# Parity attention: a power moved behind the first copies, z weight loads in step 0, output products from step 8

## The chip, the cores and the metric

The kernel runs on one core of a Trainium2 chip. The metric is device time in microseconds, the median of the runs shown. Engines: TensorE (PE), VectorE (DVE), ScalarE (ACT), GpSimd (POOL) and SyncE (SP). SP and POOL here also issue most of the DMAs, each in the order of its own instructions; ACT issues a few.

## The reference, cut to what matters

x has 2048 rows of 576 numbers (bf16). Four layers, A B A B, each adds its result to x:

```python
# A: 32 heads of 18; position p sees p, p-2, ..., p-14
qkv = layernorm(x) @ wqkv
attn = softmax(mask(q . k[p - 2w], w = 0..7) * 18**-0.5)
x = x + (attn @ v) @ wo
# B: gMLP
z = gelu(layernorm(x) @ w_in)                 # 576 -> 4608, halves z1, z2
g = w_sp @ layernorm(z2) + b_sp               # mixes the 2048 rows
x = x + (z1 * g) @ w_out
```

## The kernel before

The rows of x are handled by parity: even rows first, then odd rows, so that attention at distance 2 is attention at distance 1. Row block i has 128 rows; there are NS = 16.

**Layer A** (`layer_A`, L332) has a preparation and a loop of NST = 34 steps. Everything in it is written in order by hand (`manual_schedule`, L363): each engine, and SP and POOL as DMA queues, carries out its instructions in the order in which the code names them.

- Preparation, first layer (li = 0, L554 to L670): per row block S_ takes mean and variance on DVE, R_ (L594) adds epsilon on DVE and takes the power -1/2 on POOL (L597), A_ (L600) normalises on DVE, T_ (L615) transposes into xnT by a DMA on SP (T_pe: on PE for the first four). VW (L391) makes a piece of V. PG (L402) makes one projection of q or k for 128 columns d and 512 rows cc; it goes to a staging buffer, and when a buffer (d, 1024 rows) is complete, 8 copies by DMA (L439) put its heads into QK. `queues` tells which of SP and POOL issues a copy: they take turns for d = 0 and 4, and POOL has two of three for the others (q2, L551). In the first layer the staging of d = 3 and 4 for the first 1024 rows is borrowed from `win2a` (lent, L362), into which the z weights are loaded later. `fill_window_rows` (L194) writes the window pattern into QK on DVE.
- Before the loop come six more PG (`pre`), L_mm(0), EXP(0) and, in the first layer, two VW (L750 to L759).
- Step s of the loop (L760) does L_mm(s+1) (logits of half of a tile's heads, PE), EXP(s+1) (ACT, L462), PV(s) (PE, L476; then DVE L482, L483), and then what a table holds for step s. Tile t has two steps, 2t and 2t+1. There are 17 tiles: 128 rows, then 120 each. After the second step the tile's output o_t is transposed by a DMA on SP: odd tiles and tile 0 straight into the ring oT (L489), the other even tiles into a slot (L493), from which O_CP (L502, DVE) copies into the ring.
- The table is filled by `at(step, function)`, and within a step the order is that of the calls. PG and VW that are left; O_CP; XO (loads the residual rows, SP); WO(i, half) (output product, PE L530; addition, DVE L533); LN_STATS and LN_XN (statistics on DVE, then POOL: L231, L232, L252, L255); XST and XN_ST (stores of x and of the normalised rows, SP); LN_T (loads rows transposed into xnT, SP, L549; two for each block i from 8 on).
- `lag`, `twice` and `units` (L717 to L720) say in which steps the WO halves stand: one in each step from `lag` on, two in the steps of `twice`. `wo_steps[i]` are the two steps of block i; O_CP, XO, LN_STATS and so on get their steps from it (L722 to L740). `vsteps` (L712) are the steps of the VW that are left.
- In the first layer the output weights wo (`load_wo`, SP) are loaded in step 2 and the first three quarters of the z weights (`load_win2a`, six pieces, POOL) in steps 3, 5, ..., 13 (L741 to L744). The rest, win2b, goes in steps 16 to 26 (POOL).

In the third layer (li = 2) wqk, wv, wo and win2a are already loaded during the layer before.

**Layer B** (`layer_B`, L778) makes z2 by row blocks from xnT (z_mm, L836), then the gate products (L984) and the output products (L1033). Its first z products stand on PE among the last WO of layer A.

Of the kernel before, what the change touches and what calls it, by code (L numbers as in the profile page):

```python
# [63 lines left out]
class K:  # L64
# [267 lines left out]
    def layer_A(self, li):  # L332
        nc, tc, cfg = self.nc, self.tc, self.cfg
# [57 lines left out]
        def VW(t, hh, dve):  # L391
            nk = tdim(t)[0]
            pv = self.PT_tile([P, 512], f32, "pv")
            for c in range(5):
                nc.tensor.matmul(pv[:nk, 0:288], lhsT=self.xnT[:, c, k0_(t):k0_(t) + nk],  # L395
                                 rhs=wv_sb[:, c, hh * 288:(hh + 1) * 288], start=(c == 0), stop=(c == 4))
            evac(v_ext[:nk, t, 16 * hh:16 * hh + 16, 0:DH], pv[:nk, 0:288].rearrange("p (b d) -> p b d", d=DH), dve)
# [43 lines left out]
        NST = 2 * NT  # L441
# [112 lines left out]
        if li == 0:  # L554
# [39 lines left out]
            def R_(i0, n):  # L594
                rs = rstds[:, i0:i0 + n]
                nc.vector.tensor_scalar_add(out=rs, in0=mvs[:, i0:i0 + n, 1], scalar1=EPS)
                nc.gpsimd.tensor_tensor(out=rs, in0=rs, in1=self.neg_half[:, 0:1].to_broadcast([P, n]), op=ALU.pow)  # L597
            xns = {}

            def A_(*tiles):  # L600
                for i in tiles:
                    xns[i] = xn = self.xn_bufs[self.xn_rr % len(self.xn_bufs)]
                    self.xn_rr += 1
                    nc.vector.tensor_scalar(out=xn[:, 0:D], in0=xts[i], scalar1=mvs[:, i, 0:1],
                                            scalar2=rstds[:, i:i + 1], op0=ALU.subtract, op1=ALU.mult)
# [54 lines left out]
            for k_, (d, cc) in enumerate(order):  # L660
                for qk in ((1, 0) if d < 4 else (0,)):
                    PG(d, qk, cc, False, (nc.gpsimd, nc.sync) if d in (0, 4) else q2)
                if k_ == 3:
                    R_(12, 4)
                    VW(3, 0, False)
                    VW(3, 1, False)
                if k_ == 4:
                    A_(12, 13, 14, 15)
            T_(12, 13, 14, 15)
            nvw0, nvw = 4, 9  # L670
# [28 lines left out]
        def at(s, f, *a):  # L699
            table.setdefault(s, []).append((f, a))  # L700
        pgs = [(d, qk, cc) for d, cc in ((0, 2), (1, 2), (2, 2), (0, 3), (1, 3), (2, 3), (3, 2), (3, 3), (4, 2), (4, 3))
               for qk in ((1, 0) if d < 4 else (0,))]
        PG_END = 14
# [4 lines left out]
        if li == 0:  # L708
            at(0, VW, *vws[0], True)
            at(13, VW, *vws[1], True)  # L710
            vws = vws[2:]
        vsteps = ([x for x in range(PG_END, NST) if x not in (18, 23, 28)] if li == 0 else  # L712
                  [x for x in range(3, NST) if x not in (18, 23, 28)])
        for k_, (t, hh) in enumerate(vws):
            assert vsteps[k_] <= 2 * t - 2 + hh
            at(vsteps[k_], VW, t, hh, vsteps[k_] >= PG_END and k_ % 2 == 0)
        lag = 10 if li == 0 else 9  # L717
        twice = (18, 23, 28, 31) if li == 0 else (18, 23, 28)
        units = [x for x in range(lag, NST) for _ in range(2 if x in twice else 1)]
        wo_steps = list(zip(units[0::2], units[1::2])) + [(NST, NST), (NST + 1, NST + 2)]  # L720
        assert len(wo_steps) == NS
# [17 lines left out]
                    at(s1 + 5, LN_T, 2 * i - NS + k_)  # L739
        at(2 * (NT - 3) + 3, O_CP, NT - 3)  # L740
        if li == 0:  # L741
            at(2, self.load_wo, nc.sync)
            for k_, f in enumerate(reversed(self.load_win2a(nc.gpsimd))):
                at(3 + 2 * k_, f)  # L744
        at(PG_END + 2, alloc_win2b)
        for k_ in range(6):
            at(PG_END + 2 + 2 * k_, win2b_piece, k_)
# [397 lines left out]
```

## Time and profile before

| | us |
|---|---|
| median of 3 runs | 1187.06 |
| lowest and highest | 1185.82, 1187.1 |
| the profiled execution, its own time | 1185.85 |
| its span | 1184.1 |

The span runs from the first to the last instruction of the profiled execution. Its PE is busy for 1166.3 us of it, DVE for 552.9, ACT for 339.6 and POOL for 281.1. The mean granted clock of PE is 0.994 of full speed. A row of a timeline names start, duration, engine, line, operation, what is written and read, how many instructions are merged, and in brackets the idle time before the first and what ended it. "SPq" and "POOL ... DMA_DIRECT2D" are instructions that issue DMAs.

### The profile page before, as it was taken

To read this page: it belongs to the slowest core of one execution; us is meant where nothing else is said; L and a number is where in the kernel's file an instruction comes from. 1 tells how busy PE (TensorE), PEld (TensorE's weight loads), DVE (VectorE), ACT (ScalarE), POOL (GpSimd) and SP (SyncE) were. 2 spreads that over 40 slices of the span, in tenths; PEclk is the share of its full clock that TensorE was granted. 3 is DMA by queue.
4 is the path that set the end of the run, shared out by engine and by line. 5 is a ranking of instruction groups with operands and counts; after the bars stand their busy time and mean duration, and the time that the engine had idled before them with its cause. 6 is when DMAs were issued, how large, how long until landed. Compare 5 with 4: busy or idle time off the path is not lost.

```text
span 1184.1 us, 20070 instructions
## 1 busy us (share of the span) xinstructions
PE 1166.3 (99%) x8258; PEld 620.1 (52%) x8258; DVE 552.9 (47%) x1137; ACT 339.6 (29%) x491; POOL 281.1 (24%) x411
## 2 busy tenths in 40 slices
PE   8899999999999999999999999999999999999998
PEld 5457544444444444447755674444444444444677
DVE  9568788432332232334554787873332233232322
ACT  5478554211101111101247884550111110111000
POOL 3559955100000000001135598550000000000000
PEclk9999899999999999999999999999999999999999
DMA  8699997000000000049636797940000000001332
GB/s 196 108 191 251 211 203 162 23 12 12 1 12 12 12 12 1 1 138 281 178 88 120 180 251 192 244 91 13 12 12 12 12 1 12 12 1 40 114 106 73
DMA packets 182800, 106.44 MB, mean 90 GB/s; under 512 B 134938, under 2 KB 164042, under 8 KB 182709
## 3 DMA queue, kind: packets, MB, share of 16 engines
q1 hardware_dynamic: 170117, 84.54, 30.6%
q0 software_dynamic: 6240, 14.88, 4.9%
q10 hardware_dynamic: 6352, 5.75, 1.6%
q8 instruction: 64, 1.05, 0.4%
q14 instruction: 27, 0.22, 0.1%
HBM read 42.40 MB, written 21.77 MB: 54 GB/s over the span
## 4 chain that ended last, share of the span: by engine, by line
PE 89%; DMA 3%; POOL 3%; DVE 3%; issue 1%; ACT 0%; DVEq 0%; POOLq 0%; SPq 0%
PE pg L984 42%; PE po L1033 12%; PE pz L836 6%; PE pz L960 6%; PE pz1s L960 6%; PE pzs L836 6%; PE pp L418 4%; PE pw L530 2%; PE pv L395 2%; PE L_ps L453 2%; POOL ln_xn L252 2%; PE O_ps L476 2%; DMA o_slot<-o_t 1%; DVE ln_st L591 1%; POOL QK L78 1%
## 5 line engine op out<-in xcount | busy, mean ns | idle before, releaser
L984 PE MATMUL pg<-Wq,Z 128*128 128x512 bf16 x2304 | 500.2, 379 | 0.0
L984 PEld LDWEIGHTS <-Z 128*128 128x128 bf16 x2304 | 225.4, 98 | 271.9
L988 DVE TENSOR_TENSOR g_tmp<-pg,ln_xn 128x512 f32<-128x512 f32 x144 | 99.6, 692 | 421.6 <-PE pg L984 421.6
L979 ACT ACTIVATE z1T<-pz 128x1024 bf16<-128x1024 f32 x36 | 34.9, 1021 | 500.2 <-PE pz L960 500.2
L78 POOL DMA_DIRECT2D wout<-in_B_w_out_dram x4 | 4.3, 1067 | 598.8 <-PE pg L984 598.8
L1033 PE MATMUL po<-wout,Z 128*128 128x288 bf16 x1152 | 141.4, 286 | 0.0
L462 ACT ACTIVATE P_sb<-L_ps 128x960 bf16<-128x960 f32 (+1 forms) x136 | 125.2, 971 | 39.4 <-PE L_ps L453 38.8
L1033 PEld LDWEIGHTS <-Z 128*128 128x128 bf16 x1152 | 112.7, 98 | 28.8
L836 PEld LDWEIGHTS <-xnT 128*128 128x128 bf16 (+1 forms) x800 | 68.2, 97 | 77.4 <-issue 9.7
L989 DVE TENSOR_TENSOR Z<-g_tmp,z1T 128x512 bf16<-128x512 f32 x144 | 99.7, 692 | 12.2
L885 DVE BATCH_NORM_STATS2 z_st<-zp 128x6 f32<-128x512 bf16 (+1 forms) x160 | 91.7, 619 | 20.8 <-ACT zp L883 20.6
L960 PEld LDWEIGHTS <-w 128*128 128x128 bf16 (+1 forms) x640 | 53.7, 97 | 74.0 <-issue 13.6
L418 PE MATMUL pp<-xnT,wqk_sb 128*128 128x512 bf16 x360 | 83.7, 383 | 2.0 <-DVE o_t L483 2.0
L252 POOL TENSOR_SCALAR ln_xn<-x_new,ln_mv,ln_rstd 128x576 bf16<-128x576 f32 x32 | 73.6, 2299 | 3.0
L1043 DVE TENSOR_TENSOR x_new<-po,xo 128x288 f32<-128x288 f32 (+1 forms) x64 | 28.8, 456 | 87.7 <-PE po L1033 83.9
L960 PE MATMUL pz<-xnT,w 128*128 128x512 bf16 (+1 forms) x320 | 66.5, 380 | 0.0
L960 PE MATMUL pz1s<-xnT,w 128*128 128x512 bf16 (+1 forms) x320 | 66.5, 379 | 0.0
L836 PE MATMUL pz<-win2a,xnT 128*128 128x512 bf16 (+1 forms) x240 | 60.4, 359 | 3.0 <-DMA xnT<-xn_rows 2.7
L78 POOL DMA_DIRECT2D QK<-stg x80 | 48.1, 604 | 52.6 <-DVE stg L387 23.6
L836 PE MATMUL pzs<-win2a,xnT 128*128 128x512 bf16 (+1 forms) x240 | 59.5, 358 | 0.0
L909 POOL TENSOR_SCALAR Z<-zp,z_mv,z_rstd 128x256 bf16<-128x256 bf16 x32 | 54.5, 1704 | 3.4
L883 ACT ACTIVATE zp<-pz 128x1024 bf16<-128x1024 f32 (+2 forms) x56 | 36.6, 720 | 62.9 <-PE pz L836 62.9
(107 smaller groups left out, 957.9 us busy)
## 6 DMA issues: line engine op xcount, KB each, us to landing
xres<-x_new SPq DMA_DIRECT2D x48, 288.0 KB
xo<-xres SPq DMA_DIRECT2D x32, 288.0 KB
wout<-in_B_w_out_dram POOLq DMA_DIRECT2D x4, 1296.0 KB, 8.1
xn_rows<-ln_xn SPq DMA_DIRECT2D x32, 160.0 KB
xo<-xres SPq DMA_DIRECT2D x8, 576.0 KB
w<-in_B_w_in_dram SPq DMA_DIRECT2D x16, 256.0 KB
QK<-stg POOLq DMA_DIRECT2D x52, 72.0 KB, 4.6
QK<-stg SPq DMA_DIRECT2D x42, 72.0 KB
```

The costliest lines, as they stand in the source:

```text
L78: return eng.dma_start(out=out, in_=in_)
L252: e.tensor_scalar(out=xn[:nrows, 0:D], in0=x_t[:nrows, :], scalar1=mv[:nrows, 0:1], scalar2=rstd[:nrows, 0:1], op0=ALU.subtract, op1=ALU.mult)
L418: nc.tensor.matmul(pp[:, :], lhsT=w, rhs=self.xnT[:, c, cc * 512:(cc + 1) * 512], start=(c == 0), stop=(c == 4))
L462: nc.scalar.activation(out=P_bufs[(2 * s + jp) % 4][:nk, :, :, 0:nq], in_=Lv[:nk, :, :, 0:nq], func=ACT.Exp, scale=scale)
L836: nc.tensor.matmul(out[:, o0:o0 + n], lhsT=self.xnT[r0:r1, c, r * P:(r + 1) * P], rhs=win2(c)[r0:r1, w0:w0 + n], start=start, stop=stop, t ...
L885: nc.vector.bn_stats(out=st[:, x // 512, :], in_=zp[:, x:x + min(512, w0 + n - x)])
L909: eng.tensor_scalar(out=Z[:, b0:b1, i, :], in0=zv[:, b0:b1, :], scalar1=mv[:, 0:1], scalar2=rstd[:, 0:1], op0=ALU.subtract, op1=ALU.mult)
L960: nc.tensor.matmul(outs[a_], lhsT=w1[r0:r1, c, sub * P:(sub + 1) * P], rhs=self.xnT[r0:r1, c, q * 512:(q + 1) * 512], start=start, stop=st ...
L984: nc.tensor.matmul(pg[:, :], lhsT=Z[:, jj, i, sub * P:(sub + 1) * P], rhs=Wq[q][:, i, :], start=(i == 0), stop=(i == NS - 1))
L988: nc.vector.tensor_tensor(out=tmp[:], in0=pg[:, :], in1=bsp[:, qs], op=ALU.add)
L989: nc.vector.tensor_tensor(out=uT(jj)[:, sub, qs], in0=tmp[:], in1=z1Ts[jj, sub][:, qs], op=ALU.mult)
L1033: nc.tensor.matmul(acc[hh], lhsT=u_rows(j, i), rhs=wouts[j // NJH][:, j % NJH, hh * 288:(hh + 1) * 288], start=(j == 0), stop=(j == NJ - 1))
```

## The change

Three edits in `layer_A`:

1. First layer: the power of row blocks 12 to 15 (R_) moves from behind the PGs of order 3 to behind those of order 5, that is behind the copies of d = 0 and d = 1, and their normalisation A_ from order 4 to order 5.
2. First layer: wo and all six pieces of win2a are loaded in step 0 and no longer in steps 2 to 13.
3. Both layers: `lag` is 8 (was 10 in the first layer, 9 in the third), and `twice` is steps 18 and 23 (was 18, 23, 28 and 31; 18, 23, 28). So the output products of block i stand in other steps, and with them O_CP, XO, the normalisation, the stores and LN_T. Step 28 takes a VW again.

The steps of the output products that come out of `wo_steps`:

| block | 0 | 1 | 2 | 3 | 4 | 5 | 6 | 7 | 8 | 9 | 10 | 11 | 12 | 13 |
|---|---|---|---|---|---|---|---|---|---|---|---|---|---|---|
| before, first layer | 10, 11 | 12, 13 | 14, 15 | 16, 17 | 18, 18 | 19, 20 | 21, 22 | 23, 23 | 24, 25 | 26, 27 | 28, 28 | 29, 30 | 31, 31 | 32, 33 |
| before, third layer | 9, 10 | 11, 12 | 13, 14 | 15, 16 | 17, 18 | 18, 19 | 20, 21 | 22, 23 | 23, 24 | 25, 26 | 27, 28 | 28, 29 | 30, 31 | 32, 33 |
| after, both | 8, 9 | 10, 11 | 12, 13 | 14, 15 | 16, 17 | 18, 18 | 19, 20 | 21, 22 | 23, 23 | 24, 25 | 26, 27 | 28, 29 | 30, 31 | 32, 33 |

```diff
                 if k_ == 3:
-                    R_(12, 4)
                     VW(3, 0, False)
                     VW(3, 1, False)
-                if k_ == 4:
+                if k_ == 5:
+                    R_(12, 4)
                     A_(12, 13, 14, 15)
...
-        vsteps = ([x for x in range(PG_END, NST) if x not in (18, 23, 28)] if li == 0 else
-                  [x for x in range(3, NST) if x not in (18, 23, 28)])
+        lag, twice = 8, (18, 23)
+        vsteps = ([x for x in range(PG_END, NST) if x not in twice] if li == 0 else
+                  [x for x in range(3, NST) if x not in twice])
...
-        lag = 10 if li == 0 else 9
-        twice = (18, 23, 28, 31) if li == 0 else (18, 23, 28)
...
         if li == 0:
-            at(2, self.load_wo, nc.sync)
-            for k_, f in enumerate(reversed(self.load_win2a(nc.gpsimd))):
-                at(3 + 2 * k_, f)
+            at(0, self.load_wo, nc.sync)
+            for f in reversed(self.load_win2a(nc.gpsimd)):
+                at(0, f)
```

## The prediction

> **What bounds the kernel now.** I read the page first, then the busy times by stretch, then the timeline of one engine at a time in the places where TensorE (PE) stops. Two rows of the page's 40 slices (29.6 us each):
>
> ```profile
> PEclk9999899999999999999999999999999999999999
> DMA  8699997000000000049636797940000000001332
> ```
>
> The change touches only the two attention layers, which the timeline puts at 0 to 140 us and 601 to 719 us. The DMA engines are full in most of the first and in the second half of the other. Where PE stops there, and what it costs:
>
> ```profile
> 44.00:51.90 7.90, 6.20 (x55) 3.37 (x54) 5.92 (x6) 2.81 (x6) 4.64 (x5) 1.00 0.87 124
> 51.90:55.30 3.40, 3.40 (x51) 1.89 (x48) 1.89 (x5) 2.69 (x4) 0.00 (x0) 0.50 0.02 5
> 79.20:82.60 3.40, 3.40 (x33) 1.64 (x32) 2.10 (x7) 0.09 (x1) 2.32 (x4) 0.50 1.20 203
> 130.40:137.20 6.80, 6.12 (x42) 4.08 (x43) 2.95 (x8) 0.66 (x1) 6.33 (x8) 0.50 0.94 228
> 632.00:720.00 88.00, 85.03 (x1448) 58.02 (x1447) 63.27 (x175) 69.35 (x88) 61.10 (x81) 1.00 0.85 195
> ```
>
> Columns: stretch, its length, PE, PE weight loads, VectorE (DVE), ScalarE (ACT), GpSimd (POOL), granted clock, DMA share, GB/s. In the first attention layer the clock is at 0.50 in three stretches; each follows a PE wait shown below. The second layer (last row) keeps clock 1.00 and idles PE for only 2.97 us in 88. So the first layer has something to give, the second nearly nothing.
>
> **Part A, the power behind the first copies.** POOL, then SP, then PE at the end of the wait:
>
> ```profile
> 30.74 1.01 POOL L597 TENSOR_TENSOR lnx_rstd<-lnx_rstd,neg_half 128x4 f32<-128x4 f32 x1 [9.36 <-DVE lnx_rstd L596]
> 31.70 8.80 POOL L78 DMA_DIRECT2D QK<-stg  x15
> ```
> ```profile
> 27.70 7.71 SPq L78 DMA_DIRECT2D QK<-stg  x9
> 35.51 5.60 SPq L78 DMA_DIRECT2D QK<-win2a  x7
> 41.21 5.39 SPq L259 DMA_TRANSPOSE xnT<-ln_xn  x4
> ```
> ```profile
> 50.60 0.21 PE L453 MATMUL L_ps<-QK 32*128 32x128 bf16 x1 [1.49 <-DMA QK<-win2a]
> ```
>
> POOL sits 9.36 us in front of the power while its first copies could go: SP issues the same kind from 27.70. One copy costs 8.80/15 = 0.587 us of POOL. By the queue lists of L662, POOL has 4 copies of column block 0 and 5 of block 1. After the change these 9 run from 27.70 to 32.98, the power to 33.99, and the other 15 start at 33.99 instead of 31.70 + 9 x 0.587 = 36.98: 2.99 us earlier. The last of them is what PE waits for at 50.60. What gets later: the power by 2.2 us, and behind it on DVE the four normalisations and the eight V evictions (L687). PE can run four PSUM tiles ahead of those, so I price that at under 0.5 us; it falls into time in which PE would wait for copies anyway. What is late next: the four transposes on SP, 41.21 to 46.60, which do not move and which the first projection of the loop needs. They cap the gain. I take **-2.5**. Ends: -4.7 (all 2.99, and the half-clock stretch from 51.90, worth half of 3.40, does not occur) and +1.0 (PE waits for the V evictions and nothing is returned).
>
> **The loads in step 0.** Six POOL issues, about 0.6 us each like the copies, come right behind POOL's last copy, and two SP issues come behind the four transposes. By the shapes they carry 6 x 288 + 648 = 2376 KB; at the last table row's 195 GB/s that is 12.5 us of DMA. POOL and the DMA engines are empty at 51.90 to 55.30 (0.00 busy, share 0.02), so this work moves into a hole and leaves the full stretch after it. Two of the pieces wait for the borrowed staging buffers to be copied out, as they do now; behind them on POOL stand only the copies of step 2. I take 0 for the issues themselves; what the traffic does is in A's cap and in B.
>
> The Trainium skill, "DMA: Bandwidth & Descriptors", section "Issuing engines are not separate DMA queues", says that DMAs of all issuing engines end on the same 16 DMA engines and interleave. It speaks against this edit: loads started from POOL would slow the SP transposes that A is capped by, and the share of 0.87 at 44.00 to 51.90 agrees that there is little room before the hole. By it A would be near 0; that is the second rival.
>
> **Part B, the stop in steps 10 and 11.** The chain of work, then PE:
>
> ```profile
> 69.27 8.90 DMA o_slot<-o_t
> ```
> ```profile
> 76.27 0.56 PE L476 MATMUL O_ps<-v_ext,P_sb 128*128 128x19 bf16 x16
> 78.78 1.92 PE L418 MATMUL pp<-xnT,wqk_sb 128*128 128x512 bf16 x5 [1.95 <-DVE o_t L483]
> ...
> 82.37 0.58 PE L476 MATMUL O_ps<-v_ext,P_sb 128*128 128x19 bf16 x16
> ...
> 84.94 0.56 PE L476 MATMUL O_ps<-v_ext,P_sb 128*128 128x19 bf16 x16
> ```
>
> L476 opens each step. The step with the wait takes 6.10 us, the next of the same content 2.57: 3.53 lost, of it 1.95 in the wait and the rest at half clock (79.20 to 82.60). The cause is the slot transpose issued at 69.27, which needs 8.90 us in a full DMA. With wo's two issues gone from SP ahead of it and the z weights gone from its traffic, it leaves SP some 4 us earlier and lands sooner. Against it: the output products start two steps earlier, so the copy out of this slot (L502) comes in step 9, not 10. I take **-3.0**, ends -3.5 and +1.0.
>
> The Trainium skill, "TensorE: Matmul & The Clock Gate", section "HAM oscillation — how this bites in real kernels", states the rule as no PE gaps over about 3.4 us. The gap of 1.95 us here, with a clock of 0.50 right after it, does not agree that shorter gaps are free. By the page's rule B would be the wait alone, -1.95; I go by the row.
>
> **Part C, the end of the first layer.** PE there, and the same place in the second layer:
>
> ```profile
> 127.81 0.57 PE L476 MATMUL O_ps<-v_ext,P_sb 128*128 128x19 bf16 x16
> 131.09 0.61 PE L836 MATMUL pz<-win2a,xnT 128*128 128x512 bf16 x1 [2.71 <-DMA xnT<-xn_rows]
> ...
> 133.19 0.63 PE L476 MATMUL O_ps<-v_ext,P_sb 128*128 128x19 bf16 x16
> ...
> 139.65 0.59 PE L836 MATMUL pz<-win2a,xnT 128*128 128x512 bf16 x2
> ```
> ```profile
> 710.55 0.57 PE L476 MATMUL O_ps<-v_ext,P_sb 128*128 128x19 bf16 x16
> ...
> 713.09 0.56 PE L476 MATMUL O_ps<-v_ext,P_sb 128*128 128x19 bf16 x16
> ...
> 718.29 0.77 PE L530 MATMUL pw<-wo_sb,oT 128*128 128x288 bf16 x5 [1.00 <-DVE x_new L533]
> 718.90 0.59 PE L836 MATMUL pz<-win2a,xnT 128*128 128x512 bf16 x2
> ```
>
> The last two loop steps are 5.38 apart in the first layer and 2.54 in the second, and the rest to the gMLP products takes 6.46 against 5.81: 2.84 + 0.65 = 3.49 to be had. PE waits for the normalised rows of block 8, whose output product moves from steps 24, 25 to 23, and whose normalisation on POOL comes earlier with the whole chain (two z loads also leave POOL's queue in it). But SP's order changes here:
>
> ```profile
> 122.88 0.34 SPq L78 DMA_DIRECT2D xn_rows<-ln_xn  x1
> 123.27 1.29 SPq L78 DMA_DIRECT2D xres<-x_new  x1
> 124.66 1.34 SPq L493 DMA_TRANSPOSE o_slot<-o_t  x1
> 126.05 0.58 SPq L78 DMA_DIRECT2D xres<-x_new  x1
> 126.81 2.55 SPq L549 DMA_TRANSPOSE xnT<-xn_rows  x2
> ```
> ```profile
> L252 POOL TENSOR_SCALAR ln_xn<-x_new,ln_mv,ln_rstd 128x576 bf16<-128x576 f32 x32 | 73.6, 2299 | 3.0
> ```
>
> Now the slot transpose of tile 14 goes ahead of the pair into xnT. The pair moves from step 30 to 28 and the slot stays in step 29, so it stands behind them, and they wait until the block's rows have landed (122.88 to 126.81, 3.93). From the end of that normalisation the slot transpose leaves at 3.93 + 2.55 = 6.5 and lands some 5 to 6 later, at 11 to 12.5. I walk POOL from step 9 at about 3.5 us a block (2.30 for L252 plus its small operations) and put that end 1.2 us before step 28; DVE wants the slot in step 31, about 9.8 after it at 2.2 us a step. That is a new wait of 1.2 to 2.7; I take 1.5. C is -3.49 + 1.5 = **-2.0**, ends -3.5 and +3.0.
>
> **Part D, steps left with little on PE.** Steps 30 and 31 of the first layer and 31 of the second lose half their filling.
>
> ```profile
> 127.69 1.83 ACT L462 ACTIVATE P_sb<-L_ps 128x960 bf16<-128x960 f32 x2 [0.25 <-PE L_ps L453]
> ```
>
> Such a step cannot be shorter than ACT's 1.83 + about 0.2; its PE work, once one product (0.7) is taken from a step of 2.3, is 1.6. Three times 0.4 is **+1.2** (ends 0.5 and 1.5); the work taken out goes to steps 8 and 9, which PE bounds.
>
> **Part E, copies out of the slots two steps after the transpose.** The only one so close now is tile 12 in the second layer:
>
> ```profile
> 702.74 0.79 PE L530 MATMUL pw<-wo_sb,oT 128*128 128x288 bf16 x5 [0.62 <-DVE oT L502]
> ```
>
> Tile 10 joins it in both layers and tile 12 in the first: three places at 0 to 0.62, **+1.0** (ends 0 and 3). At the end of the second layer the reordering of SP costs about 1 as in C, and the 1.00 of 718.29, a wait for late residual rows, can go: **0**, ends -2 and +2.
>
> **Sum.** -2.5 - 3.0 - 2.0 + 1.2 + 1.0 + 0 = -5.3 against the profiled execution's 1185.85 (its span 1184.1 and 1.75 around it). That execution is 1.2 under the median, 1187.06, so I carry the difference over: 1187.06 - 5.3 = **1181.8**.
>
> **Rivals.** First, **SP's queue decides (slower)**. If the normalisation of block 8 ends one block (3.5 us) later against the loop than I walked it, the pair into xnT holds the tile 14 slot back that much longer, in both layers: +7.0, and 1.7 for one more half-clock stretch: 1181.8 + 8.7 = 1190.5. It beats my gains from a delay of about 2.7 in each layer. For it: POOL is 93% busy from 130.40 to 137.20 (6.33 of 6.80). Against it: the chain starts two steps earlier. Second, **the loads take back what the copies gain**: the loads collide with the last transposes, or POOL's first copies are held by something else and the edit does not do what it says (A at 0), and the slot in step 9 still waits 1.9: 1181.8 + 2.5 + 1.9 = 1186.2. For it: share 0.87 before 51.90. Third, **all waits go**: A at -4.2 and C at -3.5: 1181.8 - 1.7 - 1.5 = 1178.6.
>
> **How the numbers follow.** Forecast 0.50, third rival 0.16, second 0.20, first 0.14. A measurement of this kernel can tell about 0.2% (2.4 us) from no change, so the first two cases count as faster (0.66), the second rival as the same (0.20), the first rival as slower (0.14). Range: the terms' ends do not all fall together, so below I stop at 1176, somewhat under the third rival; above at 1189.5, between the two bad rivals, which leaves most of the first one out. The forecast's own range is 1178.5 to 1184.5.
>
> **What would show it.** A: POOL's first copy near 27.7, the power near 34, PE's wait before 51 gone or under 0.7. B: no wait of over 1 us in steps 8 to 12 and clock 1.00 there. C: the wait at L836 gone, a shorter one for L502 in step 31 or 32. D: ACT without gaps in steps 30 to 33. E: short waits at L530 near step 24. I am wrong if the second layer gets more than 2 us longer, or if a stop in steps 8 to 12 stays with its half clock.

## The result, and the profile after

The kernel before takes 1186.73 us (median of 13 runs, 1180.65 to 1190.03), the changed kernel 1181.71 us (median of 13). One of these 13 took 1989.8 us at a granted clock of 0.556 and is left out of the ratio; the other 12 lie between 1176.17 and 1186.24, with a median of 1180.86. The ratio is **0.9955, with a 95% interval of 0.9934 to 0.9975**: 5.3 us faster by the ratio (5.0 by the medians), where 5.3 were forecast. The two profiled executions are 1185.85 and 1182.76 us long (spans 1184.1 and 1181.0), 3.1 apart. Executions of either kernel spread over 10 us, so one pair of traces shows which waits there are, and the medians say what they are worth.

The starts of the loop's steps, taken from the L476 rows of PE's timeline in both traces:

| place | before | after | after - before |
|---|---|---|---|
| first layer, step 0 | 51.59 | 47.99 | -3.60 |
| step 2 | 56.31 | 58.86 | +2.55 |
| step 11 | 76.27 | 80.92 | +4.65 |
| step 12 | 82.37 | 83.46 | +1.09 |
| step 30 | 123.39 | 123.69 | +0.30 |
| step 31 | 125.47 | 128.67 | +3.20 |
| step 33 | 133.19 | 133.23 | +0.04 |
| second layer, step 0 | 633.28 | 631.54 | -1.74 |
| step 33 | 713.09 | 711.33 | -1.76 |
| gMLP products behind it | 718.90 | 715.99 | -2.91 |

The gain of 3.1 is a small rest of large moves in both directions. The clock in the 40 slices of the page of the changed kernel:

```profile
PEclk9899999999999999999999999999999999999999
```

The lowest clock of the first slices is now in the second (29.5 to 59 us, 8), and no longer in the fifth. What happens there is in the timelines of POOL, SP and PE of the changed kernel and in its chain of waits:

```profile
28.64 5.32 POOL L78 DMA_DIRECT2D QK<-stg  x9 [6.93 <-DVE QK L202]
33.99 1.03 POOL L597 TENSOR_TENSOR lnx_rstd<-lnx_rstd,neg_half 128x4 f32<-128x4 f32 x1
...
44.20 2.30 POOL L78 DMA_DIRECT2D win2a<-in_B_w_in_dram  x3
47.46 2.99 POOL L78 DMA_DIRECT2D win2a<-in_B_w_in_dram  x3 [0.96 <-DMA QK<-win2a]
```
```profile
41.65 5.24 SPq L259 DMA_TRANSPOSE xnT<-ln_xn  x4
```
```profile
45.65 10.31 DMA xnT<-ln_xn
```
```profile
36.93 2.61 PE L395 MATMUL pv<-wv_sb,xnT 128*128 128x288 bf16 x20 [1.03 <-DVE v_ext L387]
...
56.10 0.59 PE L418 MATMUL pp<-xnT,wqk_sb 128*128 128x512 bf16 x1 [5.07 <-DMA xnT<-ln_xn]
```

POOL starts its copies 3 us sooner, ends them sooner, and so starts the z loads at 44.20, when SP has not yet issued the last of its four transposes. That last one (45.65) needs 10.31 us to land, and PE waits 5.07 us for it. There is a smaller price of the same edit before that: the power comes later, with it the normalisation and the V evictions on DVE (L387), and PE waits 1.03 us for one of these (first row of PE); the trace of the kernel before has no such wait. The busy times by stretch of the changed kernel (columns as in the prediction) show what follows:

```profile
51.70:61.94 10.24, 5.62 (x57) 2.32 (x58) 1.75 (x5) 1.95 (x3) 0.00 (x0) 0.51 1.02 187
74.00:82.00 8.00, 7.89 (x128) 4.76 (x129) 6.62 (x18) 5.45 (x7) 1.84 (x5) 1.00 1.03 151
126.80:130.20 3.40, 3.29 (x42) 1.91 (x42) 1.17 (x3) 1.39 (x2) 3.15 (x5) 0.54 1.04 256
```

Half clock for 10.24 us where before it was 3.40. But steps 10 and 11 (second row) have no stop and a clock of 1.00; step 11 to 12 takes 2.54 us, not 6.10:

```profile
78.37 0.56 PE L476 MATMUL O_ps<-v_ext,P_sb 128*128 128x19 bf16 x16
80.92 0.56 PE L476 MATMUL O_ps<-v_ext,P_sb 128*128 128x19 bf16 x16
83.46 0.56 PE L476 MATMUL O_ps<-v_ext,P_sb 128*128 128x19 bf16 x16
```

At the end of the first layer the stop has moved from step 32 to step 30. PE, then SP, the chain and POOL of the changed kernel:

```profile
123.69 0.56 PE L476 MATMUL O_ps<-v_ext,P_sb 128*128 128x19 bf16 x16
126.91 1.29 PE L530 MATMUL pw<-wo_sb,oT 128*128 128x288 bf16 x5 [2.66 <-DMA oT<-o_t]
128.67 0.60 PE L476 MATMUL O_ps<-v_ext,P_sb 128*128 128x19 bf16 x16
131.01 0.57 PE L476 MATMUL O_ps<-v_ext,P_sb 128*128 128x19 bf16 x16
133.23 0.55 PE L476 MATMUL O_ps<-v_ext,P_sb 128*128 128x19 bf16 x16
```
```profile
119.69 0.34 SPq L78 DMA_DIRECT2D xn_rows<-ln_xn  x1
120.08 0.42 SPq L78 DMA_DIRECT2D xres<-x_new  x1
120.61 1.31 SPq L489 DMA_TRANSPOSE oT<-o_t  x1
122.02 4.56 SPq L549 DMA_TRANSPOSE xnT<-xn_rows  x2
```
```profile
120.61 6.26 DMA oT<-o_t
```
```profile
117.07 2.29 POOL L252 TENSOR_SCALAR ln_xn<-x_new,ln_mv,ln_rstd 128x576 bf16<-128x576 f32 x1
119.43 0.24 POOL L255 COPY ln_xn<-ln_xn 128x64 bf16<-128x64 bf16 x1
```

The same transpose on SP in the kernel before:

```profile
119.55 1.31 SPq L489 DMA_TRANSPOSE oT<-o_t  x1
```

Step 32 to 33 takes 2.22 instead of 5.38: the wait at the z products is gone. Step 30 to 31 takes 4.98 instead of 2.08: PE waits for the transpose of tile 13. SP could issue that only at 120.61, behind the store of block 8's rows (119.69), which waits for POOL's normalisation (it ends at 119.43 + 0.24 = 119.67). In the kernel before, the transpose stood ahead of that store (119.55 against 122.88), and the output product that reads it, block 12's, stood in step 31 and not in step 30. 3.16 were won and 2.9 lost.

### The profile page after: what moved, and what is told of

It is laid out like the page before. It is cut to its first block, busy times and chain, and to the rows that moved or that the text cites. A ratio compares the mean times of both kernels' runs of the same rounds, so it can differ in the third digit from the quotient of the medians.

```text
span 1181.0 us, 19973 instructions
## 1 busy us (share of the span) xinstructions
PE 1156.3 (98%) x8161; PEld 618.1 (52%) x8258; DVE 554.1 (47%) x1137; ACT 339.4 (29%) x491; POOL 281.1 (24%) x411
## 4 chain that ended last, share of the span: by engine, by line
PE 92%; DMA 3%; DVE 2%; issue 1%; ACT 1%; SPq 1%; POOL 1%; DVEq 0%; ACTq 0%; POOLq 0%
PE pg L983 42%; PE po L1032 12%; PE pz L959 6%; PE pz L835 6%; PE pz1s L959 6%; PE pzs L835 6%; PE pp L418 4%; PE pw L530 3%; PE pv L395 3%; PE L_ps L453 2%; PE O_ps L476 2%; DMA xnT<-ln_xn 1%; SPq L78 1%; ACT P_sb L462 1%; DMA oT<-in_A_x_dram 1%
## 5 line engine op out<-in xcount | busy, mean ns | idle before, releaser
L418 PEld LDWEIGHTS <-wqk_sb 128*128 128x128 bf16 x360 | 33.5, 98 | 42.0 <-issue 6.8
```

Source lines behind the costliest of these rows:

```text
L418: nc.tensor.matmul(pp[:, :], lhsT=w, rhs=self.xnT[:, c, cc * 512:(cc + 1) * 512], start=(c == 0), stop=(c == 4))
```

## The experiments

My first theory, from the pair of traces: the loads in step 0 cost the copies' gain, and the two other edits bring the 5 us. All ratios are against runs of the kernel before on the same chip, five rounds each. Experiments 1 to 4, 5 to 8, 9 to 11 and 12 ran on four chips, so across these groups the ratios are to be compared, not the times.

**1. The copies alone.** The kernel before with only this:

```
                 if k_ == 3:
-                    R_(12, 4)
                     VW(3, 0, False)
                     VW(3, 1, False)
-                if k_ == 4:
+                if k_ == 5:
+                    R_(12, 4)
                     A_(12, 13, 14, 15)
```

> The kernel before with only the power (and the four normalisations) moved behind the first copies. Theory (the copies' gain is real, and in the changed kernel the loads of step 0 take it back): step 0 starts 3.6 us earlier as in the changed kernel, nothing else collides with the four SP transposes, PE waits less than 1 us in steps 1 and 2, and about 3 us of it reach the end: 1183 to 1184, ratio 0.997. Rival (the gain would be lost in any case, since the stop of steps 10 and 11 takes it up: the slot transpose comes into a DMA that is just as full): 1186 to 1187, ratio 1.000.

Measured: 1184.09, ratio 0.9983 (0.9964 to 1.0002): -2.0 us of 1186, between the two. In its trace step 0 starts at 48.95 (-2.6), and the lead is still 2.95 at step 10. The lead is in the trace; in the medians, alone, it is at the edge of what can be told from nothing.

**2. The loads alone.**

```
-            at(2, self.load_wo, nc.sync)
-            for k_, f in enumerate(reversed(self.load_win2a(nc.gpsimd))):
-                at(3 + 2 * k_, f)
+            at(0, self.load_wo, nc.sync)
+            for f in reversed(self.load_win2a(nc.gpsimd)):
+                at(0, f)
```

> The kernel before with only the loads moved to step 0. Theory: the four SP transposes land late beside 2.4 MB of loads, PE waits 3 to 6 us in step 1 with a half clock behind it, steps 10 and 11 lose their stop (-3.5): between 1186 and 1190, ratio 1.000 to 1.003. Rival (the loads are the main gain of the change, because they take away the stop of steps 10 and 11, and the wait in step 1 is caused by the copies that come earlier): no wait over 2 us in step 1, 1183 to 1184, ratio 0.997.

Measured: 1181.99, ratio 0.9967 (0.9951 to 0.9984): **-3.9 us**. The theory fell. POOL of this kernel:

```profile
49.24 3.06 POOL L78 DMA_DIRECT2D win2a<-in_B_w_in_dram  x3
54.72 1.60 POOL L78 DMA_DIRECT2D win2a<-in_B_w_in_dram  x3 [2.43 <-issue]
```

With the power ahead of the copies the loads come 5 us later than in the changed kernel, behind the transposes; PE has no wait over 1 us in step 1, and step 11 to 12 takes 2.54 (78.06 to 80.60), so the stop of steps 10 and 11 is gone with this edit alone.

**3. The output products alone** (`lag, twice = 8, (18, 23)` for both layers; power and loads as before).

> The kernel before with only the output products moved (start in step 8, two in steps 18 and 23). Theory: the end of the first layer gets 3 to 5 shorter, that of the second 1 to 3, a new wait of 1 to 3 for tile 13's transpose in step 30; the stop of steps 10 and 11 stays about as long: 1182 to 1184, ratio 0.997. Rival (the earlier products need the earlier loads): the copy of the slot is due a step earlier while its transpose still stands behind wo's issues and in the z traffic, the stop grows by 2 to 4 with a longer half clock and eats the gain: 1185 to 1187, ratio 1.000.

Measured: 1189.90, ratio 1.0039 (1.0021 to 1.0058): **+4.6 us, slower**, worse than either expected. The chain of waits names the cause:

```profile
72.65 9.41 DMA o_slot<-o_t
```

The slot's transpose lands only at 82.06, and its copy is due a step earlier than before: step 10 takes 7.35 us to step 11, and that 4.21 to step 12.

**4. The changed kernel without the loads edit** (copies and products moved).

> The changed kernel with the loads back where they were before (wo in step 2, one z piece in each of steps 3, 5, ... 13). Theory: no wait over 1 us in step 1, so 4 to 7 us are won by step 8, and the stop of steps 10 and 11 comes back (3.5 to 5): 1179 to 1182, a little below the changed kernel (1181.7), ratio 0.994. Rival (the early loads are needed by the early products): the stop is longer than what step 1 gives, 1184 to 1187, ratio 0.998 to 1.000.

Measured: 1186.33, ratio 1.0018 (1.0001 to 1.0034). The rival is right in kind. Chain and PE:

```profile
67.84 11.87 DMA o_slot<-o_t
```
```profile
80.14 1.38 PE L530 MATMUL pw<-wo_sb,oT 128*128 128x288 bf16 x5 [5.84 <-DVE oT L502]
```

Without the early loads the slot needs 11.87 us, and one step takes 9.60. So the second theory: the loads in step 0 are the main gain, the products can't do without them, and the copies, which bring the loads beside the transposes, are bad company for them.

**5. Copies and loads, products as before.**

> The kernel before with the copies and the loads moved, the products as before. New theory (copies and loads are bad company: POOL, done 3 us sooner with its copies, issues the first z loads at 44 and not at 49, so that they stand beside the four SP transposes): PE waits 4 to 5.5 us in step 1 with a long half clock, as in the changed kernel; steps 10 and 11 have no stop: 1184 to 1186.5, ratio 0.999 to 1.000, slower than the loads alone (1182.0). Rival (the edits add up, -1.5 for the copies and -3.6 for the loads): 1180.5, ratio 0.9957.

Measured: 1177.91, ratio **0.9940 (0.9920 to 0.9961)**, by the ratios 1.8 us below the changed kernel, though the intervals overlap. The second theory fell too: the two edits add up at the least, -7.1 against -2.0 - 3.9. POOL, PE and the chain:

```profile
43.66 2.64 POOL L78 DMA_DIRECT2D win2a<-in_B_w_in_dram  x3
```
```profile
52.65 2.29 PE L418 MATMUL pp<-xnT,wqk_sb 128*128 128x512 bf16 x5 [1.69 <-DMA xnT<-ln_xn]
...
127.80 0.61 PE L836 MATMUL pz<-win2a,xnT 128*128 128x512 bf16 x1 [3.39 <-DMA xnT<-xn_rows]
```
```profile
116.12 2.31 POOL ln_xn L252
118.75 4.25 DMA xn_rows<-ln_xn
123.07 4.69 DMA xnT<-xn_rows
```

The z loads start just as early as in the changed kernel, and here PE waits 1.69 in step 1 and not 5.07. Up to step 2 the two kernels have the same instructions. So the same collision has a different price from one execution to another (the last transpose lands after 7.06 us here and after 10.31 there), and one trace shows one of these prices. The wait at the end of the layer is back (3.39), and its chain begins with POOL's normalisation.

**6. Loads and products, copies as before** (the power ahead of the copies).

> The changed kernel with the power back ahead of the copies. New theory: no wait over 2 us in step 1, no stop in steps 10 and 11, and the end of the first layer 3 to 5 shorter, with the wait of 1 to 3 for tile 13's transpose in step 30: 1177 to 1180, 2 to 4 below the changed kernel, ratio 0.994. Rival (the edits add up, and the copies are worth 1.5 here too): 1183, ratio 0.998.

Measured: 1182.59, ratio 0.9971 (0.9955 to 0.9986). The rival, that the copies are worth 1.5 here too, fits: 0.9971 - 0.9955 = 0.0016, 1.9 us, with nearly 3 us to either side. Its trace has no wait over 0.5 us in steps 0 to 2, one of 1.56 for a copy ahead of the loop, and one of 2.10 for tile 13's transpose.

The seven combinations with the loads on POOL, as ratios:

| | products as before | products moved |
|---|---|---|
| neither | 1 | 1.0039 |
| copies | 0.9983 | 1.0018 |
| loads | 0.9967 | 0.9971 |
| copies and loads | 0.9940 | 0.9955 |

In us (x 1186): the copies bring 1.9 to 3.2 in every row, the loads 3.9 to 8.1, and the products cost 4.2 to 4.6 without the loads and 0.5 to 1.8 with them. An interval is about 2 us to either side, that of a difference nearly 3. So the loads' gain and the products' cost without the loads are clear of zero; the copies' gain is carried by the agreement of four rows, and the last two numbers can't be told from zero.

**7. The loads behind the transposes, in step 2.** The changed kernel with

```
-            at(0, self.load_wo, nc.sync)
+            at(1, self.load_wo, nc.sync)
             for f in reversed(self.load_win2a(nc.gpsimd)):
-                at(0, f)
+                at(2, f)
```

> The changed kernel with wo loaded in step 1 and all six z pieces in step 2. New theory (the loads have only to stay out of the way of the four SP transposes and to be through before the slot transpose of step 9): no wait over 1 us in step 1, step 8 some 6 to 7 us earlier than in the changed kernel, no stop of over 1.5 us in steps 8 to 11: 1174 to 1178, ratio 0.990 to 0.993. Rival (the loads must be in step 0: from step 2 on the z traffic runs beside the copies of steps 2 to 6 and the slot transpose of step 8 as without the edit): a stop of 3 to 6 us in steps 9 to 11, 1182 to 1186.

Measured: 1183.22, ratio 0.9979 (0.9965 to 0.9993): no better than the changed kernel; the rival. Step 8 did start 7.5 us earlier than in the changed kernel (65.74), and step 9 to 10 then took 9.17. Chain, SP and PE:

```profile
60.14 16.71 DMA xo<-in_A_x_dram
```
```profile
66.44 12.01 SPq L78 DMA_DIRECT2D QK<-stg  x4
```
```profile
77.45 0.58 PE L476 MATMUL O_ps<-v_ext,P_sb 128*128 128x19 bf16 x16 [4.98 <-DVE x_new L533]
```

Now it is not the slot but the residual rows (xo), issued at 60.14 behind the z loads of 57.76, that need 16.71 us; SP needs 12.01 us to issue four copies, for which it needs 3.27 at other times.

**8. One z piece in each of steps 1 to 6** (`at(1 + k_, f)`, wo in step 1).

> The changed kernel with wo in step 1 and one z piece in each of steps 1 to 6. New theory: as with all of them in step 2, or up to 2 us worse, since the last piece lands only about step 7 to 8 and POOL's copies stand between: 1174 to 1180. Rival (the loads must be in step 0): a stop in steps 9 to 11, 1182 to 1186.

Measured: 1181.56, ratio 0.9963 (0.9945 to 0.9981), as fast as the changed kernel. The number fits neither line well, the mechanism is the rival's: the slot again, as in experiment 4, and a step of 6.64.

```profile
64.90 10.89 DMA o_slot<-o_t
```

So the loads have a narrow place: behind the four transposes, and ahead of what SP sends in steps 2 to 8.

**9. Copies and loads, with the later z loads (win2b, steps 16 to 26) issued by SP.** Experiment 5 with

```
-            pieces.extend(self.load_win2b(nc.gpsimd))
+            pieces.extend(self.load_win2b(nc.sync))
```

> Copies and loads moved, products as before, and the six later z loads (win2b, steps 16 to 26) issued by SP and not by POOL. Theory (the wait of 3.39 us for the normalised rows at the end of the first layer is POOL's queue, 3.55 us a block, with 0.65 more for each z load in it): block 8 is normalised about 3.3 us earlier, PE's wait for the rows falls below 1 us, the half clock behind it goes, the last two loop steps are 2 to 4 apart and not 6.07: 1174 to 1176, ratio 0.991 to 0.992 (copies and loads alone: 0.9940). Rival (the wait is set by the output product's step, as the change assumes, or the DMAs of the rows are what is slow): the wait stays over 2.5 us and the time at 1178, ratio 0.994.

Measured: 1177.21, ratio 0.9941 (0.9921 to 0.9961). The mechanism is the theory's, the time the rival's. PE:

```profile
38.48 4.28 PE L395 MATMUL pv<-wv_sb,xnT 128*128 128x288 bf16 x20 [2.16 <-DVE v_ext L387]
...
122.77 0.56 PE L476 MATMUL O_ps<-v_ext,P_sb 128*128 128x19 bf16 x16
123.77 0.38 PE L836 MATMUL pz<-win2a,xnT 128*128 128x512 bf16 x1 [0.44 <-ACT P_sb L462]
125.24 0.56 PE L476 MATMUL O_ps<-v_ext,P_sb 128*128 128x19 bf16 x16
```

The wait for the rows has gone; step 32 to 33 takes 2.47, not 6.07, without any output product moved. In the trace of experiment 5 the end of the layer was bound by **POOL's queue**: 3.55 us for each block, some 0.65 more with a z load in it. But the median gained only 0.7 us and the ratio nothing. Part of the puzzle is which executions were traced: that of experiment 5 took 1182.75 us, 4.8 above its kernel's median, and this one 1175.36, the fastest of its nine. So the wait of 3.39 with the half clock behind it need not be in the usual execution; how often it is stays open. This trace pays elsewhere: PE waits 2.16 us for a V eviction before the loop (first row; the same 20 matmuls took 2.61 us in the changed kernel and take 4.28 here), step 0 starts at 51.21, no earlier than in the kernel before, and step 1 has no wait over 0.53.

**10. The changed kernel with the later z loads by SP.**

> The changed kernel with the six later z loads issued by SP. Theory for the new wait of tile 13's transpose in step 30 (2.66 us; its landing takes 6.26 us in a DMA with a share of 1.26, in which the rows of block 8, z pieces and the pair into xnT travel with it): POOL's blocks move up by 3 us, the rows and the pair no longer fall on the same stretch, the wait shrinks by 1 to 2.5: 1178 to 1180, ratio 0.992 to 0.994. Rival (that transpose always stands behind the rows of block 8 and the residual store on SP, and now behind a z load as well): the wait stays or grows, 1181 to 1183, ratio 0.996 to 0.998.

Measured: 1175.22, ratio 0.9930 (0.9904 to 0.9955). The wait in its trace is the rival's; the time lies below both lines. The traced execution is the slowest of the seven (1182.06; the next is 1178.11), so its waits can't be taken for those of the median:

```profile
117.63 6.29 DMA oT<-o_t
```
```profile
123.96 0.79 PE L530 MATMUL pw<-wo_sb,oT 128*128 128x288 bf16 x5 [2.18 <-DMA oT<-o_t]
```

Here POOL began block 8 at 111.21, 2.97 us ahead of step 27 (in the changed kernel 0.04 behind its start), and the transpose still left SP 3.45 us after the start of that step: here SP was late by its own work, one issue behind the other from 114.95 on.

**11. Copies and loads, all z loads by SP.** Experiment 9 (the expectation calls it the "first kernel of this call"), and in step 0

```
-            for f in reversed(self.load_win2a(nc.gpsimd)):
+            for f in reversed(self.load_win2a(nc.sync)):
```

> As the first kernel of this call, and the six z pieces of step 0 issued by SP too, behind the four transposes and wo. Theory (what costs in step 1 is that POOL starts the z loads at 44 us, while SP's transposes are still being issued): with all transposes issued first, PE's wait in step 1 (1.69 with copies and loads moved, 5.07 in the changed kernel) falls below 1 us, 1 to 3 less than the first kernel of this call: 1172 to 1175, ratio 0.989 to 0.991. Rival (the DMA engines mix the transfers however late the loads are issued, since the transposes need up to 10 us to land): the wait is the same 1.5 to 5, and the first slot transposes on SP get later, 1175 to 1179.

Measured: 1174.34 (1173.13 to 1176.58), ratio **0.9915 (0.9891 to 0.9938)**. The number is the theory's, and so is the step: no wait over 0.52 in step 1. SP, then the busy times by stretch:

```profile
42.10 5.20 SPq L259 DMA_TRANSPOSE xnT<-ln_xn  x4
47.36 1.18 SPq L78 DMA_DIRECT2D wo_sb<-in_A_wo_dram  x2
48.58 3.46 SPq L78 DMA_DIRECT2D win2a<-in_B_w_in_dram  x6
```
```profile
44.00:56.00 12.00, 11.32 (x168) 6.59 (x168) 9.68 (x17) 8.76 (x12) 1.81 (x4) 1.00 0.98 261
70.00:82.00 12.00, 11.95 (x211) 7.84 (x211) 9.96 (x28) 9.14 (x10) 7.16 (x11) 1.00 0.64 150
110.00:125.00 15.00, 14.37 (x253) 10.89 (x252) 12.89 (x41) 11.09 (x14) 13.70 (x17) 1.00 0.86 228
```

The z loads leave behind the last transpose. PE is busy nearly throughout and the clock is 1.00 in all three places that had a stop. The executions also lie closer together: 3.5 us from the fastest to the slowest of 6. Against experiment 9, on the same chip, the median is 2.9 us lower and five of the six executions are faster than all nine of that one, though the intervals of the ratios overlap.

The trace of experiment 9 doesn't show this gain in step 1, since there the time was lost before the loop. The traces that do show it are those that start step 0 within 0.8 us of one another. With the loads on POOL, step 0 starts at 47.92 (experiment 5) and 47.99 (the changed kernel), and step 2 at 55.41 and 58.86. With the loads on SP, step 0 starts at 48.47 here and at 48.66 in experiment 12, and step 2 at 52.75 and 53.06.

**12. The changed kernel with all z loads by SP.**

> The changed kernel with all z loads issued by SP: those of step 0 behind the four transposes, the later ones in steps 16 to 26. It differs from the best kernel so far (copies and loads moved, all z loads by SP, products as before: 1174.34, ratio 0.9915) only in the output products. Theory (the products of the change cost, and don't gain, once the waits they were to remove are gone otherwise: two products more in steps 8 and 9, and the wait of 2.2 to 2.7 us for tile 13's transpose with its half clock): no wait over 1 us in step 1, the wait in step 30 stays, 1176 to 1179, ratio 0.993 to 0.996, 2 to 4 slower than that kernel. Rival (the earlier products still gain what the profile of the change shows at its end, 1.7 in the first layer and 2.9 in the second): 1171 to 1174, ratio 0.989 to 0.991.

Measured: 1174.00 (1172.93 to 1176.38), ratio **0.9891 (0.9867 to 0.9915)**, the best of all; the theory's wait in step 30 isn't there. Chain and PE:

```profile
112.36 5.25 DMA oT<-o_t
118.92 2.66 DMA o_slot<-o_t
```
```profile
118.80 0.56 PE L476 MATMUL O_ps<-v_ext,P_sb 128*128 128x19 bf16 x16
121.06 0.56 PE L476 MATMUL O_ps<-v_ext,P_sb 128*128 128x19 bf16 x16
122.97 0.55 PE L476 MATMUL O_ps<-v_ext,P_sb 128*128 128x19 bf16 x16
```

Tile 13's transpose leaves SP 2.40 us after the start of step 27 (109.96), against 3.58 in the changed kernel (120.61 - 117.03) and 3.45 in experiment 10 (117.63 - 114.18), and lands a microsecond sooner. Against experiment 11 the medians differ by 0.3 and the ratios by 0.0024 with overlapping intervals: whether the products gain anything with the queues in order stays open. The two intervals allow a cost of about 1 us at most, so one of 2 to 4 is excluded. Both kernels beat the kernel before; the interval of the last lies wholly below that of the change, that of experiment 11 overlaps it by 0.0004.

## Why the prediction was right, point by point

The sum was right (-5.3 for -5.3 by the ratio), and three of its places were, but not all its terms; that it came out to the tenth is luck (below).

- **A, the copies (-2.5): right in size.** The table gives -1.9 to -3.2. POOL's first copy ran at 28.64, not 27.7, since POOL first waits for DVE (L202), and so the power at 33.99, a microsecond after the 32.98 of the sum. The cap by the four transposes is what the trace shows. The second rival's mechanism, loads that collide with the last transposes, was there too (5.07 us and 10.24 us at half clock in the profiled execution), but its consequence, A at nothing, was not: by the medians the collision costs less, and the order of experiment 11 removes it without bringing the stop of steps 10 and 11 back. One term of A was too small: PE's wait for the V evictions, priced at under 0.5. It is 1.03 in the changed kernel and 0.50 to 2.31 in nine of the ten traces with the power moved; the four traces with the power in its old place have none. In experiments 9 and 10 (2.16 and 2.31, with half clock behind them) step 0 started at 51.21 and 51.52, where the kernel before has 51.59: in these executions it is the bad end of A, nothing returned.
- **The loads (0 for the issues) and B (-3.0): right.** The stop in steps 10 and 11 is 3.56 us shorter in the traces, and the loads alone bring 3.9. Only the "some 4 us earlier" out of SP was too much: the slot's transpose left at 71.84, 1.44 us ahead of step 8, and before at 69.27, 0.17 ahead of it, so 1.3. It landed sooner: its copy ran at 78.13 without a wait, at most 6.3 us after the issue, where it took 8.90. What I put "against it", that the copy out of the slot is due a step earlier, is the reason why the products lose 4.6 without the loads.
- **C (-2.0 = -3.49 + 1.5): the place right, the new wait misjudged.** The old wait went (3.16). In place of 1.5 the new one cost 2.9, half clock included, and it isn't the one I named: PE waits for tile 13's transpose, not DVE for tile 14's slot. The step that failed is the walk of SP's order: it followed tile 14's slot and the pair ahead of it, and left out that tile 13's transpose is now behind block 8's store too, and that the product which reads it stands a step earlier. POOL adds to it: I put the end of block 8's normalisation 1.2 us before step 28; it ended at 119.67, 0.4 after (step 28 starts at 119.27), and SP, free from 118.43 on, stood until then. But POOL alone is not the cause: in experiment 10 it was 3 us earlier, and the wait was 2.18 all the same. In experiment 12 the transpose left 2.40 after the start of step 27 and landed in 5.25, and the wait was 0.48. This is akin to the first rival (POOL's end holds up a transpose on SP), with 1.6 us instead of 3.5, another transpose, and in the first layer only.
- **D (+1.2): the mechanism seen, the size too large.** Steps 30 and 31, which lost work, are no shorter for it (2.19 and 2.26 in experiment 12, 2.19 and 2.23 in experiment 11), and steps 8 and 9, where work went, are 0.5 and 0.3 longer. But step 32 is 0.6 shorter (1.91 against 2.48), so that steps 8 to 32 together take only 0.3 more (56.77 against 56.49).
- **E (+1.0): not seen.** The trace of the changed kernel has no wait of 0.3 or more for L502 in either layer.
- **The second layer (0, -2 to +2):** it starts 1.74 earlier and its last products 2.91 earlier, so -1.2. The wait of 1.00 for late residual rows, which I said could go, is gone.

Two errors cancel. A and B were forecast at -5.5 together, and the table gives -7.1 for copies and loads; C + D + E was forecast at +0.2, that is, that the moved products gain nothing by themselves, and the table gives +1.8 for them beside copies and loads. Each of these has an interval of 2 to 3 us, so the agreement to the tenth is luck; that the sum is about -5 is not. On "DMA: Bandwidth & Descriptors", section "Issuing engines are not separate DMA queues", of the Trainium skill: its rule that the transfers of all issuing engines interleave agrees with the 10.31 us of the last transpose; by my rival drawn from it A would have been lost, and the runs decide against that size.

## What to carry to other kernels

Loads that were moved to a free stretch belong on the queue that carries the urgent transfers, right behind these: then they start after them, whichever engine gets ready early. Where an engine issues DMAs between computations that set the pace (POOL here), count those issues as its work. An edit that makes something due earlier is to be tried together with, and without, the edit that brings its data earlier: the products alone were 4.6 us slower, with the loads they cost nothing that could be measured. And a trace is one execution: see where it lies among the times of its kernel before its waits are taken for those of the median.

## What the runs showed of the hardware that I had not expected

- The time of a transfer isn't fixed by its size. A tile's transpose into a slot landed 2.66 us after its issue in experiment 12 (tile 14, at a DMA share of 0.90), 8.90 in the kernel before and 11.87 in experiment 4 (both at 1.13). A load of residual rows took 16.71 (also at 1.13).
- SP's own issue slows down: four copies took it 12.01 us beside six z loads (experiment 7, DMA share 1.09), and 3.27 in the kernel before (58.79 to 62.06, share 0.39).
- The clock falls after waits that I would have thought harmless, but the length of a wait alone doesn't decide it. In the attention layers of all fourteen traces (from 14 us on), every wait of PE of 2.10 us or more had a stretch at 0.50 behind it, and the 5.07 one of three times the length (10.24 us). Of the shorter ones some had it (1.44 in experiment 8, 1.51 in experiment 4, 1.69 in experiment 5) and some stayed at 1.00 (1.48 in experiment 4, 1.83 in experiment 12, 2.00 in experiment 1); none of about 1 us had it. Where it comes, a stretch of 3.4 us at half clock costs 1.7. The rule that the prediction quotes from the Trainium skill, "TensorE: Matmul & The Clock Gate", section "HAM oscillation — how this bites in real kernels" (no gaps over some 3.4 us), would call most of these waits harmless; the rows decide.
